# Attention's products with v and the state as moving operand, and chunk 0's w, k, r in 1,536-byte packets

## The chip, the cores and the metric

The kernel runs on one core of a Trainium2 chip. The metric is device time in microseconds, of the one core from launch to end; less is better. A core has TensorE (PE in the profile; PEld is its loading of the stationary operand, here called a load), VectorE (DVE), ScalarE (ACT), GpSimd (POOL) and SyncE (SP), which here sends the DMAs. Engines run side by side and wait for each other at semaphores. On each engine the instructions stand in a fixed order, written when the program is built.

In a product on TensorE one operand is loaded into the array and stays (stationary), the other streams through it (moving). In the profile's shapes `a<-m,v 128*64 128x128` the first pair is the loaded operand, rows by columns, and the second is the result's or the moving operand's, partitions by columns.

## The reference

An attention with a decaying state (4 batches, 8 heads, 768 tokens, head size 48), and an FFN with a squared ReLU on its result (3,072 tokens, 384 to 2,048 to 384), all in float32:

```python
for t in range(S):
    kt, vt, rt, wt = (k[:, :, t], v[:, :, t], r[:, :, t], w[:, :, t])
    cur = np.einsum('bhd,bhe->bhde', u[None] * kt, vt)
    y[:, :, t] = np.einsum('bhd,bhde->bhe', rt, state + cur)
    state = wt[:, :, :, None] * state + np.einsum('bhd,bhe->bhde', kt, vt)
...
x = np.ascontiguousarray(attn_out.transpose(0, 2, 1, 3)).reshape(B * S, H * D)
h = np.maximum(x @ w_in, 0.0)
return (h * h @ w_out).astype(np.float32)
```

## The kernel before, in words

**Tiling.** The 768 tokens of each batch are cut into 6 chunks of 128 (`C`). A *unit* is one chunk of one batch: 24 units, 4 a chunk. Heads go in 4 pairs (`NP`); in the layout "head dims on partitions" the pair's first head lies on partitions 0 to 47 and the second on 64 to 111 (`J` = 64, `D` = 48, `HP` = 112). Behind each chunk of attention comes the FFN of its 512 tokens: 16 steps of 128 hidden columns each. A step has 9 products with w_in (`hp`, L640; three products of rounded halves for each of 3 row blocks), a squared ReLU with a split into two rounded halves (ACT and DVE, L645 to L649), and 3 products with w_out for each batch (`ob`, L655). The first 6 steps of chunk 0 and all of chunk 1 are done in two halves of 2 batches.

**A unit.** (1) w, k, r arrive with tokens on partitions (`st`, L423) and must be turned. In chunk 0 that is four transposes a tensor on TensorE (`turn`, L466), in the later chunks a block transpose on DVE (L432) and DMAs that spread the blocks (L442). (2) DVE multiplies the decays up along the tokens (`scan`, L478) and, with ACT's reciprocal (L485, L486), scales r (L489) and k (L495 to L498). (3) `beta`, the sum over a head of u k r for each token, comes from two products on POOL (L505, L507) and a sum on DVE (L508); ACT writes it onto the diagonal of `m` (L515). (4) TensorE makes the scores of 128 by 128 tokens for each head (L526), DVE copies their causal part into `m` (L530). (5) The *mix* makes y: state times r (`inter`, L552) and v times scores (`part`, L560), summed in one PSUM tile `a`. v or the state is loaded (48 columns, or 64 with 16 of the head before), and 128 columns of r or scores move, so y comes out with head dims on partitions and the tokens along the row, as the FFN needs x. (6) ACT and DVE split y into the rounded halves of x (L591, L592). (7) The new state: k is turned to tokens (`ktok`, L538, L540), multiplied with v (`outer`, L611; 64 or 48 columns of k loaded, 48 columns of v moving) and added (L617 to L620).

Four pairs of 96 head dims must become three tiles of 128 rows. Pair 1 is therefore split: its dims are put on the 16 free partitions at either side of the other three pairs. In chunk 0 a copy `ly` (L577) and products with 0/1 matrices (`sel`, L574) do that on TensorE, later a tile `x3` and six DMAs for two units (`send`, L599). Rows of w_in are loaded in the same order, in five pieces a group (L370).

**Weights.** w_in and w_out come in 8 groups (`ri`, `ro`: 768 KB each) and are split into two rounded halves on the chip: ACT (L383, L403), DVE (L387, L391, L396) and POOL (L404).

**What sets the order.** The class `Plan` simulates the engines with the costs that stand in each `P.add(...)` and writes out an order for each engine; `Ranks` holds tables of numbers by which it prefers one step to another. Where the plan expects TensorE to be idle in the first 110 us, it puts in transposes of the unit matrix (L681) that keep its clock up. PSUM has 8 banks: 4 for the outputs `ob`, 2 for `hp`, 2 for `a`. In chunk 0 the `ob` and `hp` banks hold turned w, k, r as well.

Of the kernel before, what the change touches and what calls it, by code (L numbers as in the profile page):

```python
# [35 lines left out]
class Plan:  # L36
# [9 lines left out]
    LANES, RUNS, SLACK, START = 8, 2300, 2.0, 2.4  # L46
# [142 lines left out]
class Ranks:  # L189
    AT = {'load': -105.75, 'z': 279.5, 'pt': 293.75, 'rk': -330.75, 'beta': 21.25, 'far': 18.25, 'v': 60.25, 'scan': 43, 'ln': 19.75, 'rt': 19.5, 'kn': 51, 'diag': -5.25, 'mt': -159, 'mask': 173.5, 'ktp': -201.5, 'kt': 16.25, 'mix': 5.25, 'x': -131, 'x3': -22.5, 'send': 36, 'dS': 23, 'S': 10.5}  # L190
    AT0 = {'load': -89.75, 'turn': 101.5, 'rk': -33, 'beta': 11.5, 'far': 133.25, 'v': -15.75, 'scan': -196.25, 'ln': -291, 'rt': -31, 'kn': 99.25, 'diag': 45.5, 'mt': -172.75, 'mask': -100.5, 'ktp': 40.25, 'kt': 29.25, 'mix': -212, 'x': 187.5, 'x3': 11, 'send': 93, 'dS': -48, 'S': -101}
    AT1 = {'load': -20.75, 'z': -9.75, 'pt': -57, 'rk': -13, 'beta': 104.5, 'far': 35.25, 'v': -5.75, 'scan': -5.25, 'ln': -68, 'rt': -39.75, 'kn': 2, 'diag': 120.5, 'mt': -311.5, 'mask': -60.25, 'ktp': -46.5, 'kt': -83, 'mix': -111.75, 'x': -6.75, 'x3': -270.75, 'send': -105.75, 'dS': -29.75, 'S': 8.75}
    U0 = (-64.5, -118.75, -8.75, -25)
    C1 = (9.25, 16.75, 53.25, 46)
    W0 = (-110.25, -66.25, -12, 2.25, 3.25, 5, 8.25, 20)
    WL = (-20.5, 13, -41.5, -13, -1, 8.75, 20, 11.5)
    OFF = {'hp': 2.75, 'g': -5.75, 'ob': 4, 'os': 64.5}
    LAG = 2
# [25 lines left out]
def kernel(  # L224
# [46 lines left out]
    PC = J - D  # L271
    TILES, SPLIT = (0, 2, 3), 1
    SIDE = ((0, 0), (2, 1), (1, 2))
    spare, spare2 = placed[f"ro{NG - 2}"], placed[f"ri{NG - 2}"]
    sel = place("sel", [HP, KT, J], F32, spare)
    last_y = [place(f"ly{i}", [HP, C], F32, spare + 768 + 512 * i) for i in range(2)]
    first_v = [place(f"v0{i}", [128, H * J], F32, at) for i, at in enumerate((spare + 1792, spare + 3840, spare2, spare2 + 2048))]
# [28 lines left out]
    for t in st0:  # L306
        V.memset(t[:, :, :, :, D:J], 1.0)
# [34 lines left out]
    for t in first_v:  # L342
        V.memset(t.rearrange("s (h x) -> s h x", h=H)[:, :, 0:PC], 0.0)
# [4 lines left out]
    for t in Ss:  # L348
        V.memset(t, 0.0)
# [436 lines left out]
```

## Time and profile before

| | |
|---|---|
| median of 3 runs | 549.76 us (549.22 to 550.37) |
| the profiled execution | 549.26 us, of which 547.3 us are its span |
| granted TensorE clock, mean | 0.996 |
| DMA | 206,456 packets, 50.88 MB; 196,161 of them under 512 bytes |
| POOL in the first 40 us | busy between 0 and 4.7 us of each 5 |

A row of groups names the line, the engine, the operation, the tiles (out<-in, buffer numbers left out), the shapes and the count; behind the first bar stand the busy time in us (overlaps counted once) and the mean duration of one in ns, behind the second the idle time of the engine ahead of these instructions and what ended it. A row of the timeline has start and length in us, then a run of like instructions with its count. Records of TensorE overlap: one lasts some 200 to 400 ns, while the next starts well before it ends. A float32 product is two records for each instruction of the program; the FFN's products and the transposes are one.

### The profile page before, as it was taken

To read this page: it belongs to the slowest core of one execution; us is meant where nothing else is said; L and a number is where in the kernel's file an instruction comes from. 1 tells how busy PE (TensorE), PEld (TensorE's weight loads), DVE (VectorE), ACT (ScalarE), POOL (GpSimd) and SP (SyncE) were. 2 spreads that over 40 slices of the span, in tenths; PEclk is the share of its full clock that TensorE was granted. 3 is DMA by queue.
4 is the path that set the end of the run, shared out by engine and by line. 5 is a ranking of instruction groups with operands and counts; after the bars stand their busy time and mean duration, and the time that the engine had idled before them with its cause. 6 is when DMAs were issued, how large, how long until landed. Compare 5 with 4: busy or idle time off the path is not lost. (4 is left out here: it accounts for less than half of the span.)

```text
span 547.3 us, 10350 instructions
## 1 busy us (share of the span) xinstructions
PE 532.6 (97%) x3930; PEld 474.5 (87%) x3930; DVE 357.1 (65%) x650; ACT 287.3 (52%) x677; POOL 102.3 (19%) x119
## 2 busy tenths in 40 slices
PE   7899999999999999999999999999999999999995
PEld 6778988889998989888888888888888889899994
DVE  5889989999587775958667747656855332333331
ACT  2886885566855845655643654545553332332322
POOL 5335653540212020210302002003000000000000
PEclk9999999999999999999999999999999999999998
DMA  9999699156563825455553723703411000000001
GB/s 164 216 244 272 128 245 206 24 90 136 115 132 64 169 47 105 97 104 99 101 107 62 138 73 60 142 3 73 74 57 30 1 0 16 29 31 1 0 1 62
DMA packets 206456, 50.88 MB, mean 93 GB/s; under 512 B 196161, under 2 KB 201281, under 8 KB 206401
## 3 DMA queue, kind: packets, MB, share of 16 engines
q1 hardware_dynamic: 205680, 49.17, 44.0%
q10 hardware_dynamic: 720, 0.98, 0.6%
q8 instruction: 33, 0.54, 0.4%
q14 instruction: 23, 0.18, 0.1%
HBM read 31.65 MB, written 4.72 MB: 66 GB/s over the span
## 5 line engine op out<-in xcount | busy, mean ns | idle before, releaser
L655 PE MATMUL ob<-wo,g 128*128 128x384 f32 x1152 | 226.9, 341 | 0.5 <-ACT g L648 0.5
L640 PE MATMUL hp<-x,wi 128*128 128x512 f32 (+1 forms) x1062 | 222.7, 355 | 1.4 <-DVE g L649 0.9
L655 PEld LDWEIGHTS ob<-wo,g 128*128 128x128 f32 x1152 | 199.3, 188 | 9.2 <-ACT g L648 0.7
L640 PEld LDWEIGHTS hp<-x,wi 128*128 128x128 f32 x1062 | 174.5, 188 | 27.5 <-DVE g L649 2.3
L645 ACT ACTIVATE t<-hp 128x512 f32<-128x512 f32 (+1 forms) x118 | 61.1, 518 | 154.2 <-PE hp L640 132.5
L646 DVE SCALAR_TENSOR_TENSOR hp<-hp,t 128x512 f32<-128x512 f32 (+1 forms) x118 | 70.3, 596 | 102.0 <-ACT t L645 101.5
L649 DVE TENSOR_TENSOR g<-hp,g 128x512 fp32r<-128x512 f32 (+1 forms) x118 | 68.9, 585 | 38.1 <-ACT g L648 37.3
L648 ACT CAST g<-hp 128x512 fp32r<-128x512 f32 (+1 forms) x118 | 59.5, 505 | 55.7 <-DVE hp L646 55.6
L515 ACT ACTIVATE m<-ident,beta 128x128 f32<-128x128 f32 x192 | 60.4, 395 | 1.2 <-DVE beta L508 1.2
L505 POOL TENSOR_TENSOR st<-st 128x384 f32<-128x384 f32 x24 | 26.6, 1108 | 61.7 <-DVE st L432 54.5
L620 POOL TENSOR_TENSOR S<-S,Ec 112x192 f32<-112x192 f32 x16 | 8.3, 523 | 142.2 <-DVE S L619 142.2
L530 DVE COPY_PREDICATED m<-caus,a 128x512 f32<-128x512 uint8 x48 | 33.3, 730 | 0.7 <-PE a L526 0.6
L478 DVE TENSOR_TENSOR_SCAN pt<-pt,zero 112x128 f32<-112x128 f32 x80 | 30.3, 426 | 3.0 <-DMA v<-in_v_dram 1.3
L526 PEld LDWEIGHTS a<-pt 48*128 48x128 f32 x384 | 23.6, 187 | 7.3 <-issue 5.1
L526 PE MATMUL a<-pt 48*128 48x128 f32 x384 | 28.3, 285 | 1.1 <-DVE pt L498 1.1
L560 PE MATMUL a<-m,v 128*48 128x128 f32 (+1 forms) x384 | 27.2, 279 | 1.0 <-DVE m L530 1.0
L432 DVE STREAM_TRANSPOSE st<-st 128x1152 f32<-128x1152 f32 x20 | 27.2, 1366 | 0.0
L560 PEld LDWEIGHTS a<-m,v 128*48 128x48 f32 (+1 forms) x384 | 20.0, 128 | 6.4 <-issue 4.6
L592 DVE SCALAR_TENSOR_TENSOR x<-a,x 112x128 fp32r<-112x128 f32 (+2 forms) x44 | 17.5, 431 | 12.3 <-ACT x L591 11.7
L507 POOL TENSOR_TENSOR st<-st,un 128x384 f32<-128x384 f32 x24 | 25.1, 1047 | 1.6
L404 POOL TENSOR_TENSOR wi<-q,wi 128x768 fp32r<-128x768 f32 x8 | 17.6, 2204 | 38.0 <-ACT wi L403 31.5
L495 DVE TENSOR_TENSOR pt<-pt,m 112x512 f32<-112x512 f32 x24 | 17.4, 728 | 8.9 <-ACT m L486 8.3
(78 smaller groups left out, 417.1 us busy)
## 6 DMA issues: line engine op xcount, KB each, us to landing
pt<-st SPq DMA_DIRECT2D x80, 96.0 KB, 2.3
ro<-in_moe_w_out_dram SPq DMA_DIRECT2D x8, 768.0 KB, 7.5
v<-in_v_dram SPq DMA_DIRECT2D x24, 192.0 KB, 3.4
st<-in_w_dram SPq DMA_DIRECT2D x11, 384.0 KB, 4.2
st<-in_k_dram SPq DMA_DIRECT2D x11, 384.0 KB, 5.4
st<-in_r_dram SPq DMA_DIRECT2D x11, 384.0 KB, 5.6
pt<-st SPq DMA_DIRECT2D x80, 48.0 KB, 2.5
out_dram<-q SPq DMA_DIRECT2D x20, 192.0 KB, 1.9
```

The lines of the kernel that those rows point to most:

```text
L432: V.transpose(out=zt[:, i].rearrange("a t p q i -> a t (p q) i"), in_=sv[:, :, i].rearrange("s t p q x -> s t (p q) x"))
L478: lambda p=p: V.tensor_tensor_scan(out=pt[:, 0, p], data0=src(0)[:, p], data1=zero.broadcast_to([HP, C]), initial=1.0, op0=ALU.mult, op1=A ...
L515: A.activation(mv(j)[:, p], ident, AF.Copy, scale=beta.tile[:, 2 * p + j:2 * p + j + 1])
L526: T.matmul(mts[j].tile.rearrange("s (p t) -> s p t", p=NP)[:, p], pt[js, 2, p], pt[js, 1, p], start=True, stop=True)
L530: lambda j=j: V.copy_predicated(out=mv(j), mask=caus.unsqueeze(1).broadcast_to([128, NP, C]), data=mts[j].tile.rearrange("s (p t) -> s p t ...
L560: T.matmul(ybv()[to:to + n + D, spot(p)], vt.tile[:, o - n:o + D], mv(j)[:, p], start=(c == 0 and p == SPLIT), stop=True, skip_group_check ...
L640: T.matmul(hp.tile[:, 0:n], wi[f][:, wl, kt], xT[:, kt, xl, xs], start=(m == 0), stop=(m == 3 * KT - 1))
L645: P.add("act", 0.5 if full else 0.28, rank("g"), lambda: A.activation(t(), h(), AF.Relu), r=[hp], w=[(g, 1)])
L646: P.add("dve", 0.61 if full else 0.33, rank("g"), lambda: V.scalar_tensor_tensor(out=h(), in0=h(), scalar=0.0, in1=t(), op0=ALU.max, op1=A ...
L648: P.add("act", 0.53 if full else 0.31, rank("g"), lambda: A.copy(out=hi(), in_=h()), r=[hp], w=[(g, 0)])
L649: P.add("dve", 0.61 if full else 0.33, rank("g"), lambda: V.tensor_tensor(out=lo(), in0=h(), in1=hi().bitcast(F32), op=ALU.subtract), r=[h ...
L655: T.matmul(obs[b][:, 0:DM], g.tile[0][:, gl, o:o + C], wo[f][:, wl], start=(f == 0 and m == 0), stop=(f == NF - 1 and m == 2))
```

## The change

Two parts are rebuilt, and the tables of `Ranks` are other ones.

**The mix.** `part` now loads the scores (128 rows, 128 columns) and moves v (48 columns); `inter` loads r (48 rows, 128 columns) and moves the state (48 columns). y comes out with tokens on partitions and the 384 head dims along the row, in one PSUM tile in chunk 0 and in two (one for each head of a pair) later. ACT copies it to `ys` (with the sign), TensorE turns `ys` by three transposes (`back`), and ACT and DVE split the result into x. With that the 16-partition shifts go: `sel`, `ly`, `x3`, the six DMAs, w_in's row order and its five pieces.

**Chunk 0's w, k, r.** A DMA now puts 8 tokens of one head, 1,536 contiguous bytes, on a partition (head and block of 16 on the partitions), where before each token's 192 bytes were a packet. `turn` therefore isn't a transpose: for each of the 8 tokens y and each head of a pair, 64 or 48 columns are loaded and 64 picked columns of the unit matrix move; results go to every eighth column of the turned tile. `beta` of chunk 0 is made from the turned k and r: a copy on ACT, a product on DVE, four products with u on TensorE (`sums`), and a copy on ACT. In the later chunks it stays on POOL and DVE.

```diff
-    LANES, RUNS, SLACK, START = 8, 2300, 2.0, 2.4
+    LANES, RUNS, SLACK, START = 8, 2300, 2.0, 1.4
...
-    AT = {'load': -105.75, 'z': 279.5, 'pt': 293.75, 'rk': -330.75, ...
+    AT = {'load': -95.5, 'z': 119, 'pt': 209.75, 'rk': -91.75, ...
...
-        for i, (to, src) in enumerate(pieces):
-            n = 2 * PC if i >= KT else to.shape[0]
-            P.add("sp", 0.4 if i >= KT else 0.0059 * n, rank, lambda to=to, src=src: nc.sync.dma_start(out=to, in_=src),
-                  w=[("wi", g, i)], after=before, runs=n)
+        P.add("sp", 2.4, rank, lambda: nc.sync.dma_start(out=wi_r[g], in_=w_in32[g].rearrange("(k p) x -> p k x", p=128)),
+              w=[("wi", g, 0)], after=before if g == NG - 1 else [], runs=384)
...
+            for b0 in (b, b + 1) if c == 0 else ():
+                for i, src in ((0, w), (2, k), (1, r)):
+                    def load(i=i, src=src, b0=b0):
+                        nc.sync.dma_start(out=st.tile.rearrange("s (t b x) -> s t b x", t=3, b=2)[:, i, b0 - b, 0:TB * D],
+                                          in_=src[b0, :, ss, :].rearrange("h (a s) d -> h a (s d)", s=TB))
...
-                    for p in range(NP):
-                        T.transpose(out=to[:, p], in_=pairs[:, p], identity=ident)
-                P.add("pe", 0.5, rank("turn"), turn, r=[(st, ui, i)], w=[ps[i]])
+                    pick = ident.rearrange("s (p j x) -> s p j x", p=NP, j=2)
+                    for y in range(TB):
+                        for j in range(2):
+                            n = (J, D)[j]
+                            T.matmul(to[j * J:j * J + n, :, :, y], rows[:, y * D:y * D + n], pick[:, :, j], start=True, stop=True, skip_group_check=True)
+                P.add("pe", 1.0, rank("turn"), turn, r=[(st, ui, i)], w=[ps[i]], mode=3)
...
+        if c == 0:
+            P.add("act", 0.53, rank("rk"), lambda: A.activation(pt[:, 2], src(2), AF.Copy, scale=-1.0), r=keys(2), w=[PT[2]])
+            P.add("dve", 0.62, rank("rk"), lambda: V.tensor_tensor(out=pt[:, 2], in0=pt[:, 2], in1=src(1), op=ALU.mult), r=keys(1), w=[PT[2]])
+            def sums():
+                for p in range(NP):
+                    T.matmul(tl(ps[0])[:, 2 * p:2 * p + 2], pt[:, 2, p], ut[:, p], start=True, stop=True, skip_group_check=True)
+            P.add("pe", 0.45, rank("beta"), sums, r=[PT[2]], w=[ps[0]])
+            P.add("act", 0.2, rank("beta"), lambda: A.copy(out=beta.tile, in_=tl(ps[0])[:, 0:H]), r=[ps[0]], w=[beta])
...
-                    T.matmul(ybv()[j * J:j * J + n + D, spot(p)], Ss[b][js, PC + p * D - n:PC + p * D + D], pt[js, 1, p],
-                             start=(spot(p) == 0), stop=False, skip_group_check=True)
+                    T.matmul(place_of(p, j), pt[js, 1, p], Ss[b][js, p * D:p * D + D], start=(p == 0), stop=False, skip_group_check=True)
...
-                        T.matmul(ybv()[to:to + n + D, spot(p)], vt.tile[:, o - n:o + D], mv(j)[:, p],
-                                 start=(c == 0 and p == SPLIT), stop=True, skip_group_check=True)
+                    T.matmul(place_of(p, j), mv(j)[:, p], vt.tile[:, o:o + D], start=(c == 0 and o == 0), stop=True, skip_group_check=True)
...
+        if c:
+            P.add("pe", 0.45, rank("mix"), inter, r=[vt, *Ms, ("S", b), *RK], w=yb, mode=1)
+        P.add("pe", 0.75, rank("mix"), part, r=[vt, *Ms], w=yb)
...
+        def back():
+            for kt in range(KT):
+                T.transpose(out=xv()[:, kt], in_=ys.tile[:, kt * 128:kt * 128 + 128], identity=ident)
+        P.add("pe", 0.33, rank("y"), back, r=[(ys, j) for j in range(2 if c else 1)], w=[xp])
...
-                        nc.sync.dma_start(out=xT.bitcast(F32)[to:to + PC, q, :, b * C - C:b * C + C],
-                                          in_=x3.tile.bitcast(F32).rearrange("a z u c -> a z (u c)")[o:o + PC])
```

**What moves.** Lines of the changed kernel that the prediction names: L455 `turn`, L491 `sums`, L525 the scores, L550 `inter`, L556 `part`, L577 `back`, L537 `ktok`, L591 `outer`, L620 `hp`, L635 `ob`, L661 the transposes that keep the clock up; on DVE L467 the scan, L487 the product of chunk 0's `beta`, L478, L501, L502, L504 the scaling of r and k, L368, L372, L377 the weights' split, L529 the masked copy, L581 x, L597 the state.

TensorE in a steady unit, before (a are the two PSUM tiles, m the scores, v and S the values and the state, pt the scaled r and k; rows that alternate on are left out):

```order
L655 MATMUL ob_142<-wo_59,g_97 128x384 x3
L552 MATMUL a_145<-pt_127,S_130 64x128
L552 MATMUL a_145<-pt_127,S_130 48x128
...
L560 MATMUL a_145<-m_154,v_152 64x128
L560 MATMUL a_145<-m_159,v_152 48x128
...
L611 MATMUL a_146<-v_153,m_160 64x48
L611 MATMUL a_146<-v_153,m_160 48x48
...
L655 MATMUL ob_139<-wo_59,g_99 128x384 x3
```

The two mixes and the state's product stand in one block between FFN products. In the changed program, at such a unit (ys is the copied y):

```order
L635 MATMUL ob_143<-wo_67,g_94 128x384 x3
L550 MATMUL a_147<-S_128,pt_125 128x48
L550 MATMUL a_146<-S_128,pt_125 128x48
...
L620 MATMUL hp_144<-x_131,wi_73 128x512 x9
L556 MATMUL a_147<-v_154,m_159 128x48
L556 MATMUL a_146<-v_154,m_160 128x48
...
L635 MATMUL ob_140<-wo_71,g_92 128x384 x3
L635 MATMUL ob_141<-wo_71,g_92 128x384 x3
L577 MATMUL a_147<-ident,ys 128x128 x3
L537 MATMUL a_146<-ident,pt_125 128x112 x4
```

The block is taken apart, with FFN products between its pieces and ahead of the transposes that need ACT's copy; the results are 128 partitions by 48 columns instead of 64 or 48 by 128.

DVE ahead of the second unit's x, before (pt, m: decays and scaled r and k; x: the FFN's input; q: weights under way):

```order
L592 SCALAR_TENSOR_TENSOR x_134<-a_146,x_134 128x3x128
L478 SCALAR_TENSOR_TENSOR pt_128<-ob_141,zero 112x128 x4
L530 COPY_PREDICATED m_156<-caus,a_145 128x512
L530 COPY_PREDICATED m_157<-caus,a_146 128x512
L478 SCALAR_TENSOR_TENSOR pt_128<-ob_141,zero 112x128 x4
L489 TENSOR_TENSOR pt_128<-ob_142,pt_128 112x4x127
L508 TENSOR_REDUCE beta_168<-st_136 128x8
L495 TENSOR_TENSOR pt_128<-pt_128,m_155 112x512
L496 SCALAR_TENSOR_TENSOR m_155<-pt_128,m_155 112x512
L617 TENSOR_TENSOR S_129<-a_146,Ec_162 112x192
...
L592 SCALAR_TENSOR_TENSOR x_134<-a_145,x_134 128x3x128
```

Between the first unit's x and the second's stand both scans of the third and fourth unit. In the changed program:

```order
L581 TENSOR_TENSOR x_131<-a_146,x_131 128x3x128
L597 TENSOR_TENSOR S_126<-a_147,Ec_163 112x192
L368 TENSOR_SCALAR q_149<-q_149 128x768
L372 SCALAR_TENSOR_TENSOR q_149<-ri_56,q_149 128x768
L529 COPY_PREDICATED m_160<-caus,a_146 128x512
L529 COPY_PREDICATED m_161<-caus,a_147 128x512
L377 SCALAR_TENSOR_TENSOR q_149<-ri_56,q_149 128x768
L368 TENSOR_SCALAR q_148<-q_148 128x768
...
L478 TENSOR_TENSOR pt_125<-ob_143,pt_125 112x4x127
L581 TENSOR_TENSOR x_131<-a_147,x_131 128x3x128
```

There the weights' split (L368 to L377) and the third unit's scan stand between the two, and the fourth unit is not begun.

SP's first DMAs, before:

```order
L423 DMA st_135<-in_r_dram 128x8x48
L423 DMA st_135<-in_w_dram 128x8x48
L423 DMA st_135<-in_k_dram 128x8x48
L423 DMA st_135<-in_r_dram 128x8x48
L453 DMA v_91<-in_v_dram 128x8x48
L370 DMA ri_56<-in_moe_w_in_dram 112x512 x2
```

These follow the first unit's w and k; in the changed program the queue begins so:

```order
L404 DMA st_132<-in_w_dram 128x1x384
L404 DMA st_132<-in_k_dram 128x1x384
L404 DMA st_132<-in_r_dram 128x1x384
L351 DMA ri_60<-in_moe_w_in_dram 128x3x512
L353 DMA ro_62<-in_moe_w_out_dram 128x2x768
L404 DMA st_132<-in_w_dram 128x1x384
L404 DMA st_132<-in_k_dram 128x1x384
```

A group of weights, 1.5 MB, now stands ahead of the second unit's w.

More of the change, by code (lines that the diff above doesn't have):

```diff
@@ L268 @@
         wo_t.append(place(f"wo{g}", [128, 2, 2 * DM], F32R, placed[f"ro{g}"]))
[L271 to L277, printed above, removed]
+    spare = placed[f"ro{NG - 2}"]
+    first_v = [place(f"v0{i}", [128, DM], F32, spare + 4 * DM * i) for i in range(4)]
     gts = []
@@ L603, in attention @@
+        P.add("dve", 0.47, rank("x"), lambda: V.tensor_tensor(out=lo(), in0=xv(), in1=hi().bitcast(F32), op=ALU.subtract),
+              r=[xp, xk + ("hi",)], w=[xk + ("lo",)])
         if c < NC - 1:
@@ L735 @@
                     xp = pas[b % 2].rearrange("a (k s) -> a k s", s=C)[:, 0:KT]
[L737 removed]
                     for kt in range(KT):
[L739 to L744 removed]
+                        T.transpose(out=xp[:, kt], in_=xr[:, kt * 128:kt * 128 + 128], identity=ident)
                     hi, lo = (xT[:, :, z, b * C:b * C + C] for z in range(2))
```

164 lines of the change are left out of this document (61 added, 103 removed).

## The prediction

> **What bounds the kernel now.** I read the page first, then the windows of busy time, the waits of TensorE and the timeline of one steady unit; the chain that ended last came last.
>
> ```profile
> span 547.3 us, 10350 instructions
> PE 532.6 (97%) x3930; PEld 474.5 (87%) x3930; DVE 357.1 (65%) x650; ACT 287.3 (52%) x677; POOL 102.3 (19%) x119
> 1.60:34.70 33.10, 29.36 (x271) 24.71 (x271) 26.14 (x61) 20.35 (x54) 16.26 (x24) 1.00 1.11 216
> 34.70:80.00 45.30, 43.15 (x357) 38.67 (x358) 41.07 (x73) 36.71 (x87) 22.06 (x13) 1.00 0.91 213
> 80.00:420.00 340.00, 339.39 (x2653) 302.35 (x2652) 250.09 (x459) 192.66 (x472) 62.99 (x74) 1.00 0.48 95
> 420.00:540.00 120.00, 120.00 (x649) 108.15 (x648) 39.09 (x58) 35.35 (x64) 0.00 (x0) 1.00 0.03 9
> PE a L526 <- DVE pt L498: 0.3, 1, 0.3
> PE hp L640 <- DVE g L649: 0.3, 1, 0.3
> 542.41 0.48 ACT q L660
> ```
>
> The windows give, after the stretch and its length, the busy time of PE, PEld, DVE, ACT and POOL, then the granted clock (1.00 all along), the DMA share and GB/s. From 80 us on TensorE is busy in 459.39 of 460 us; the two rows of waits, taken from 80 us on, are all that it waits for, 0.6 us. So **behind 80 us the time is TensorE's own work**: whatever a unit of attention adds to TensorE comes out at the end, one for one, and nothing on DVE, ACT or the queues hides it. Before that the start is bound elsewhere: DVE has 26.14 of 33.10 us, and TensorE's 29.36 hold warming transposes of the unit matrix (L681). The chain view holds a last copy alone, since the kernel ends on a flag that is read back; it says nothing of the middle.
>
> **The change, part by part: the units behind chunk 0.** There are 20. One of them reads, on TensorE:
>
> ```profile
> 302.42 1.08 PE L552 MATMUL a<-pt,S 48*64 48x128 f32 x16
> 303.43 1.09 PE L560 MATMUL a<-m,v 128*64 128x128 f32 x16
> 304.35 0.62 PE L611 MATMUL a<-v,m 128*48 128x48 f32 x16
> 304.90 2.35 PE L655 MATMUL ob<-wo,g 128*128 128x384 f32 x12
> ...
> 314.91 1.16 PE L526 MATMUL a<-pt 48*128 48x128 f32 x16
> 316.00 0.44 PE L655 MATMUL ob<-wo,g 128*128 128x384 f32 x1
> ```
>
> Each of the 8 float32 products is two records. From start to start, L552 takes 1.01 us and L560 0.92: 1.93 us for both, and that is what goes away. In L560, v is loaded (48 or 64 columns) and 128 columns of scores move; two halves of the array work side by side. In the new form the scores are loaded (128 columns) and 48 columns of v move: **less moves, more is loaded, and no second half works beside it**. So what decides is what a load of 128 columns costs when little moves behind it.
>
> ```profile
> L611 PE MATMUL a<-v,m 128*64 128x48 f32 x160 | 12.4, 222 | 0.0
> L611 PE MATMUL a<-v,m 128*48 128x48 f32 x160 | 10.5, 210 | 0.0
> L611 PEld LDWEIGHTS a<-v,m 128*64 128x64 f32 x160 | 11.5, 138 | 1.3 <-issue 1.0 <-ACT m L540 0.2
> L611 PEld LDWEIGHTS a<-v,m 128*48 128x48 f32 x160 | 9.6, 124 | 0.0
> L694 PEld LDWEIGHTS a<-flag,ones 128*128 128x128 f32 x2 | 0.4, 188 | 0.0
> L694 PE MATMUL a<-flag,ones x2: 166/208/251, 540.4 to 540.4; 128*128 128x1 f32 x2
> 540.39 0.28 PE L694 MATMUL a<-flag,ones 128*128 128x1 f32 x2
> 12.21 4.31 PE L681 MATMUL a<-ident 128*128 128x128 f32 x38
> ```
>
> L611 is the state's product, and both its halves move the same 48 columns; one loads 64 columns, the other 48. In each of 20 units a half has 8 records, so its busy time is seven steps and one duration: (12.4/20 - 0.222)/7 = **0.057 us a step** with 64 columns loaded, (10.5/20 - 0.210)/7 = 0.045 with 48. The half that loads more is slower, so the load sets its pace, not what moves. The loads' own durations grow alike: 124, 138 and 188 ns at 48, 64 and 128 columns. L694 (the flag) is the one place where 128 float32 columns are loaded and next to nothing moves, one column: its two records are busy for 0.28 us, the first for 0.166, so the second ends 0.11 later. From 64 columns I come to the same: 0.057 + 64 x 0.012/16 = 0.105. I take **0.11 us for a record with 128 columns loaded**, however little moves.
>
> - L556, scores times v: 16 records one behind the other, 16 x 0.11 = 1.76 us. Bounds: 16 x 0.045 = 0.72, if the load were hidden, and 1.8 if each goes as a transpose of L681 does (4.31/38 = 0.113).
> - L550, r times state: 48 rows and 128 columns loaded, as L526 has them, in two row halves side by side. L526 takes 1.09 with a changeover behind it. I take 1.0; bounds 8 x 0.045 = 0.36 and 1.09.
> - L577, three transposes of the result, as L681: 3 x 0.113 = 0.34. Their wait for ACT's copy of y is covered by L635 and L620, which stand between in the order.
>
> Sum 3.10 against 1.93: +1.17 us a unit, **20 x 1.17 = +23.4 us**. By the bounds it is between 20 x (1.42 - 1.93) = -10 and 20 x (3.23 - 1.93) = +26. I stay near the upper end, since the nearest row (L694) is the very shape. Changeovers between whole and divided array are 131 and 135 in the two orders; at no more than 0.1 each that is +0.4. ACT's added copies of y and the removed DVE pieces, x3 and L599's transfers, lie beside a busy TensorE and cost or save nothing.
>
> The Trainium skill's page TensorE: Matmul & The Clock Gate has a rule that speaks for the change: by its section Back-to-back issue gap, 1 to 64 moving columns cost some 25 ns. As an estimate from that page L556 would be 16 x 0.025 = 0.4 us, L550 0.3 with its changeover, the unit 1.04 and the 20 units -18 us instead of +23.4. L611's step of 57 ns with 48 moving columns doesn't agree with it for float32 loads; it is the first rival below, priced there from rows.
>
> **The start.** What the first FFN product waits for:
>
> ```profile
> 0.82 0.45 SPq L423 DMA_DIRECT2D st<-in_w_dram  x1
> 6.08 0.89 PE L466 MATMUL ob<-ident,st 128*128 128x128 f32 x4
> 7.01 1.37 DVE L478 TENSOR_TENSOR_SCAN pt<-ob,zero 112x128 f32<-112x128 f32 x4 [2.81 <-PE ob L466]
> 7.00:35.30 28.30, 24.50 (x249) 20.03 (x248) 24.24 (x47) 20.41 (x54) 14.33 (x19) 1.00 1.15 228
> 34.71 0.38 PE L640 MATMUL hp<-x,wi 128*128 128x256 f32 x1 [0.26 <-ACT x L591]
> un<-in_u_dram ACTq DMA_DIRECT2D x1, 192.0 KB, 4.5
> out_dram<-q ACTq DMA_DIRECT2D x4, 192.0 KB, 2.3
> ```
>
> The first w is sent for at 0.82 and turned at 6.08; from the first scan (7.01) to the x of the second unit DVE has 24.24 us of work in 28.3. In the new order w comes in 128 pieces of 1,536 bytes. The nearest rows are u and the outputs, of the same size and pieces: 4.5 and 2.3 us to landing, so w lands at 3.1 to 5.3. Its turn is now 16 pairs with 64 and 48 columns loaded, at L611's 0.057: 0.91 us, where 4 transposes took 4 x 0.113 = 0.45. The first scan then starts between 4.1 and 6.4; I take 5.5, 1.5 earlier. Bounds of a turn: 16 x 0.045 = 0.72 and, if its scattered writes spoil the pairing, 32 x 0.057 = 1.8.
>
> ```profile
> L478 DVE TENSOR_TENSOR_SCAN pt<-ob,zero 112x128 f32<-112x128 f32 x16 | 5.4, 399 | 2.8 <-PE ob L466 2.8
> L530 DVE COPY_PREDICATED m<-caus,a 128x512 f32<-128x512 uint8 x4 | 2.8, 721 | 0.1
> L496 DVE SCALAR_TENSOR_TENSOR m<-pt,m 112x512 f32<-112x512 f32 x4 | 2.8, 688 | 0.1
> L592 DVE SCALAR_TENSOR_TENSOR x<-a,x 128x384 fp32r<-128x384 f32 x2 | 1.1, 558 | 1.6 <-ACT x L591 1.6
> L387 DVE TENSOR_SCALAR q<-q 128x768 uint32<-128x768 uint32 x2 | 1.1, 554 | 0.4 <-ACT q L383 0.4
> L391 DVE SCALAR_TENSOR_TENSOR q<-ri,q 128x768 uint32<-128x768 uint32 x1 | 1.0, 951 | 0.0
> ```
>
> From the first scan to the second unit's x the new order has on DVE: 12 scans (5.4/16 = 0.34), 11 products of 512 elements (0.69), 4 masks (0.72), 3 shifts (0.55), 5 bit merges (0.95), 2 x (0.56) and one state (0.36): 4.1 + 7.6 + 2.9 + 1.7 + 4.8 + 1.1 + 0.4 = 22.6 us, 1.6 less than now. With waits as now (28.3 - 24.2 = 4.1) that x, and with it the first FFN product, comes at 5.5 + 22.6 + 4.1 = 32.2, where it now is ready at 35.3 (28.3 behind 7.0): **3.1 earlier**.
>
> Behind it chunk 0 has more for TensorE than now: two turns and not one (2 x 0.91 - 0.45 = +1.4), two sums of r, k and u (L491, 8 records with 128 columns loaded, 0.88 each: +1.8), and two mixes at 1.76 + 0.34 = 2.1, where now stands
>
> ```profile
> 55.07 0.87 PE L574 MATMUL a<-ly,sel 48*64 48x128 f32 x12
> ...
> 56.57 0.62 PE L611 MATMUL a<-v,m 128*48 128x48 f32 x16
> ```
>
> 1.5 us and some 0.3 of an earlier piece: +0.6 for both. That is +3.8 against -3.1, so the start gives **+0.7**, between -4 (w lands early, waits vanish) and +7 (slow turns). The 34 warming transposes behind that point, now 25, fill waits and add none.
>
> **Sum.** The profiled execution took 549.26 us, 1.96 around its span; the median shown is 549.76, half a microsecond more, inside what I can tell. 549.3 + 23.4 + 0.4 + 0.7 = **573.8, say 574 us**.
>
> **Rivals.**
> - *The load hides behind the moving columns* (**not slower**). Were a record with 128 columns loaded as quick as L611's, 0.05, then L556 takes 0.8, L550 0.5, L577 0.34: 1.64, a gain of 0.29 a unit, 5.8 in all; the start gives -3.1 + 1.4 + 0.8 - 1.3 = -2.2. That is 549.3 - 5.8 - 2.2 + 0.4 = 542 us. It decides from a step of 0.062 us, where 24 steps, a changeover of 0.1 and the 0.34 of L577 make up the 1.93 of now. For it speaks that only two records in this trace have the new shape; against it L611's two halves.
> - *The turns are slow.* Their results go to every eighth element of PSUM, which nothing in this trace does. At 1.8 us a turn outlasts the 1.37 us of scans beside it, and from there it decides: four turns on the way to the first FFN product and two behind it, 6 x 0.9 = +5.4: 579 us. The Trainium skill's page Advanced Engine Details and Errata, section PSUM Cachelines, says that results which aren't contiguous slow matmuls significantly; no row here can show it.
> - *The start doesn't come earlier*, because the weights' large transfers stand right behind the first three and POOL and ACT are still late: the 3.1 us fall away, 577 us.
>
> **How the numbers follow.** Forecast 0.71, slow turns 0.09, no earlier start 0.06, hidden load 0.14 (of which 0.02 ends within 0.2% of now). A measurement of this kernel can tell about 0.2% from no change. So faster 0.12, same 0.02, slower 0.86. The forecast's own spread is 565 to 582 (unit sums 2.85 to 3.3, start -4 to +4); with the two slower rivals, 561 to 585 holds 0.8 and leaves out the hidden load.
>
> **What would show it.** In the new profile: L556 at about 1.8 us a unit and 0.11 a record, L550 at 1.0, L577 at 0.34; L455 at 0.9 a turn; the first L620 near 32; TensorE without waits behind 80 us. It is wrong if L556 takes under 1 us a unit, or if TensorE waits there for ACT's copies of y.

## The result, and the profile after

The changed kernel took 585.14 us (median of 4 runs, 583.16 to 586.84), the kernel before 550.07 on the same chip (549.22 to 551.24). That is 1.0635 times the time of before (95% interval 1.0594 to 1.0676): slower, as forecast, by 35 us where 24 were forecast. The profiled execution took 586.84 us, 585.1 of them its span. The profiled execution of block_inter below was a slow one (586.00 us, mean granted clock 0.987, against 577.09 to 579.76 us for its other four), so only its stretch at full clock is compared.

The windows of busy time of the changed kernel, in the columns shown for before (length, PE, PEld, DVE, ACT, POOL, granted clock, DMA share, GB/s):

```profile
1.60:34.70 33.10, 29.96 (x394) 27.74 (x394) 18.59 (x34) 17.30 (x42) 3.78 (x7) 0.95 0.81 233
34.70:80.00 45.30, 44.06 (x459) 40.56 (x458) 38.61 (x70) 33.18 (x75) 18.18 (x11) 0.96 0.79 224
80.00:420.00 340.00, 338.20 (x2510) 305.04 (x2510) 236.64 (x417) 191.14 (x477) 67.64 (x77) 1.00 0.51 81
420.00:540.00 120.00, 120.00 (x713) 107.17 (x713) 48.02 (x79) 44.51 (x92) 1.39 (x2) 1.00 0.09 23
```

and what TensorE waits for behind 80 us (in all, times, longest):

```profile
PE ob L635 <- DVE g L629: 1.0, 1, 1.0
PE hp L620 <- DVE g L629: 0.8, 1, 0.8
```

TensorE is as full as before: 338.20 of 340 us and 120 of 120, with 1.8 us of waits. More work was added to a full engine. In the first stretch POOL fell from 16.26 to 3.78 and DVE from 26.14 to 18.59, and neither made the start shorter. The clock column counts the time ahead of the first recorded change as full. That change is to full clock and came at 6.64 us before and at 19.73 after; until then the clock was half: in the changed kernel the 32 records of a turn take 1.97 us at 10.16 and 1.15 at 42.79 (both rows are below).

To see where the time came in, I count the records of the FFN's products (L620 and L635, before L640 and L655; 2,214 in both). The 200th is counted from 0 here, so 200 records lie ahead of it; behind its start 20 units of attention are left in both programs. It comes at 81.22 us before and at 92.12 after: **+10.9**. From there to the product of the flag it is 459.2 us before and 485.8 after: **+26.6**. Forecast were +0.7 and +23.8.

A later unit of the changed kernel, from its timeline on TensorE (start, length, then line, shapes and count):

```profile
296.27 2.26 PE L620 MATMUL hp<-x,wi 128*128 128x512 f32 x9
298.37 2.24 PE L635 MATMUL ob<-wo,g 128*128 128x384 f32 x12
300.45 2.26 PE L620 MATMUL hp<-x,wi 128*128 128x512 f32 x9
302.65 1.16 PE L525 MATMUL a<-pt 48*128 48x128 f32 x16
303.74 1.86 PE L635 MATMUL ob<-wo,g 128*128 128x384 f32 x9
305.53 1.09 PE L550 MATMUL a<-S,pt 48*128 48x48 f32 x16
306.56 0.80 PE L635 MATMUL ob<-wo,g 128*128 128x384 f32 x3
307.19 1.88 PE L556 MATMUL a<-v,m 128*128 128x48 f32 x16
308.89 2.35 PE L620 MATMUL hp<-x,wi 128*128 128x512 f32 x9
311.08 0.49 PE L577 MATMUL a<-ident,ys 128*128 128x128 f32 x3
311.40 0.55 PE L537 MATMUL a<-ident,pt 112*128 112x112 f32 x4
```

Starts are to be subtracted, since lengths overlap. L550 takes 305.53 to 306.56, 1.03; L556 takes 307.19 to 308.89, 1.70 (16 records, 0.106 each); L577 0.32. Together 3.05 us, where L552 and L560 took 1.93. The FFN records show a second cost. Undisturbed, 12 of L635 take 298.37 to 300.45, 2.08, so 0.173 each; the 9 ahead of L550 take 1.79 where 9 x 0.173 = 1.56, the 3 behind it 0.63 for 0.52, and the 9 of L620 behind L556 take 2.19 where undisturbed they take 2.10.

The start, first on DVE (in brackets the idle time ahead and what ended it):

```profile
6.70 1.36 DVE L467 TENSOR_TENSOR_SCAN pt<-ob,zero 112x128 f32<-112x128 f32 x4 [4.64 <-PE ob L455]
12.25 0.69 DVE L487 TENSOR_TENSOR pt<-pt,ob 112x512 f32<-112x512 f32 x1 [4.19 <-PE ob L455]
20.03 1.37 DVE L467 TENSOR_TENSOR_SCAN pt<-ob,zero 112x128 f32<-112x128 f32 x4 [1.95 <-PE ob L455]
37.77 0.56 DVE L581 TENSOR_TENSOR x<-a,x 128x384 fp32r<-128x384 f32 x1 [0.73 <-ACT x L580]
```

then on TensorE:

```profile
4.67 3.68 PE L455 MATMUL ob<-ident,st 128*64 128x64 f32 x64 [1.31 <-DMA st<-in_w_dram]
10.16 1.97 PE L455 MATMUL ob<-ident,st 128*64 128x64 f32 x32 [1.81 <-DMA st<-in_r_dram]
38.44 2.08 PE L455 MATMUL a<-ident,st 128*64 128x64 f32 x64
40.45 2.41 PE L620 MATMUL hp<-x,wi 128*128 128x256 f32 x18
42.79 1.15 PE L455 MATMUL ob<-ident,st 128*64 128x64 f32 x32
43.87 1.05 PE L491 MATMUL ob<-ut,pt 112*128 112x2 f32 x8
```

The first w is turned from 4.67 on, but the first r only from 10.16 on, so the product behind it (L487) waits 4.19 us. The second unit's x is ready at 38.33, and the first FFN product stands behind two more turns, until 40.45. At half clock two turns take 3.68 us (first row), at full clock 2.08 (third row).

### The profile page after: what moved, and what is told of

The parts are those of the page before. It is cut to its first block, busy times and chain, and to the rows that moved or that the text cites. A ratio compares the mean times of both kernels' runs of the same rounds, so it can differ in the third digit from the quotient of the medians.

```text
span 585.1 us, 10795 instructions
## 1 busy us (share of the span) xinstructions
PE 570.4 (97%) x4269; PEld 515.8 (88%) x4269; DVE 354.1 (61%) x620; ACT 298.7 (51%) x705; POOL 91.9 (16%) x104
## 5 line engine op out<-in xcount | busy, mean ns | idle before, releaser
L635 PE MATMUL ob<-wo,g 128*128 128x384 f32 x1152 | 234.2, 344 | 1.5 <-DVE g L629 1.0
L620 PE MATMUL hp<-x,wi 128*128 128x512 f32 (+1 forms) x1062 | 224.0, 356 | 1.1 <-DVE g L629 0.8
L635 PEld LDWEIGHTS ob<-wo,g 128*128 128x128 f32 x1152 | 199.1, 189 | 9.9 <-DVE g L629 1.3
L620 PEld LDWEIGHTS hp<-x,wi 128*128 128x128 f32 x1062 | 174.0, 188 | 27.0 <-DVE g L629 2.3
L556 PEld LDWEIGHTS a<-v,m 128*128 128x128 f32 x384 | 46.3, 192 | 1.0 <-DVE m L529 0.3
L556 PE MATMUL a<-v,m 128*128 128x48 f32 x384 | 46.1, 272 | 0.2 <-DVE m L529 0.2
L529 DVE COPY_PREDICATED m<-caus,a 128x512 f32<-128x512 uint8 x48 | 33.2, 733 | 13.1 <-PE a L525 10.9
L568 ACT ACTIVATE ys<-a 128x192 f32<-128x192 f32 x40 | 11.1, 330 | 51.7 <-PE a L556 51.7
L496 POOL TENSOR_TENSOR st<-st 128x384 f32<-128x384 f32 x20 | 22.1, 1107 | 79.2 <-DVE st L419 79.2
L467 DVE TENSOR_TENSOR_SCAN pt<-pt,zero 112x128 f32<-112x128 f32 x80 | 29.1, 406 | 1.4 <-DMA out_dram<-q 1.1
L525 PEld LDWEIGHTS a<-pt 48*128 48x128 f32 x384 | 23.4, 187 | 5.9 <-issue 2.4
L525 PE MATMUL a<-pt 48*128 48x128 f32 x384 | 28.0, 285 | 0.0
L581 DVE TENSOR_TENSOR x<-a,x 128x384 fp32r<-128x384 f32 x24 | 13.3, 555 | 22.6 <-ACT x L580 22.5
L550 PEld LDWEIGHTS a<-S,pt 48*128 48x128 f32 x320 | 19.4, 187 | 5.5 <-issue 3.9
L385 POOL TENSOR_TENSOR wi<-q,wi 128x768 fp32r<-128x768 f32 x8 | 16.3, 2041 | 41.2 <-ACT wi L384 41.2
```

The costliest lines, as they stand in the source:

```text
L467: lambda p=p: V.tensor_tensor_scan(out=pt[:, 0, p], data0=src(0)[:, p], data1=zero.broadcast_to([HP, C]), initial=1.0, op0=ALU.mult, op1=A ...
L525: T.matmul(mts[j].tile.rearrange("s (p t) -> s p t", p=NP)[:, p], pt[js, 2, p], pt[js, 1, p], start=True, stop=True)
L529: lambda j=j: V.copy_predicated(out=mv(j), mask=caus.unsqueeze(1).broadcast_to([128, NP, C]), data=mts[j].tile.rearrange("s (p t) -> s p t ...
L556: T.matmul(place_of(p, j), mv(j)[:, p], vt.tile[:, o:o + D], start=(c == 0 and o == 0), stop=True, skip_group_check=True)
L620: T.matmul(hp.tile[:, 0:n], wi[f][:, wl, kt], xT[:, kt, xl, xs], start=(m == 0), stop=(m == 3 * KT - 1))
L635: T.matmul(obs[b][:, 0:DM], g.tile[0][:, gl, o:o + C], wo[f][:, wl], start=(f == 0 and m == 0), stop=(f == NF - 1 and m == 2))
```

## The experiments

All of them start from the changed kernel except where it is said. The first FFN product and the 200th FFN record are starts in the profiled execution; the last column runs from there to the flag's product. Each ratio is to the kernel before on the same chip; for the runs below `after` that one took 550.55 to 551.04 us.

| kernel | median us | ratio to before (95%) | first FFN product | 200th FFN record | from there |
|---|---|---|---|---|---|
| before | 550.07 | | 34.71 | 81.22 | 459.2 |
| after | 585.14 | 1.0594 to 1.0676 | 40.45 | 92.12 | 485.8 |
| wide_v | 584.68 | 1.0560 to 1.0632 | 40.38 | 91.99 | 485.8 |
| extra_whole | 588.32 | 1.0619 to 1.0699 | 38.72 | 90.39 | 489.1 |
| extra_divided | 593.19 | 1.0746 to 1.0811 | 38.05 | 88.18 | 495.0 |
| block_inter | 579.70 | 1.0478 to 1.0538 | 40.27 | 92.29 | 483.3 |
| mix_only | 588.69 | 1.0646 to 1.0708 | 33.22 | 93.20 | 486.8 |
| loads_only | 577.23 | 1.0436 to 1.0505 | 47.23 | 107.82 | 459.2 |
| fill | 583.46 | 1.0564 to 1.0626 | 38.93 | 89.00 | 485.8 |
| late_w | 588.08 | 1.0618 to 1.0684 | 44.20 | 94.31 | 485.7 |
| late_w_fill | 590.44 | 1.0684 to 1.0742 | 43.87 | 95.59 | 485.8 |
| late_split | 588.73 | 1.0665 to 1.0707 | 45.06 | 96.73 | 485.8 |
| sums_twice | 586.01 | 1.0592 to 1.0710 | 39.73 | 91.42 | 485.8 |

The last column is the steadiest number here: 485.7 to 485.8 in six kernels whose starts differ by 8 us. It is read for the units, the two columns ahead of it for the start.

**Does the load or what moves set the pace?** Twice as many columns of v move:

```diff
-                    T.matmul(place_of(p, j), mv(j)[:, p], vt.tile[:, o:o + D], start=(c == 0 and o == 0), stop=True, skip_group_check=True)
+                    T.matmul(place_of(p, j, WV), mv(j)[:, p], vt.tile[:, min(o, DM - WV):min(o, DM - WV) + WV], start=(c == 0 and o == 0), stop=True, skip_group_check=True)
```

(WV = 96 behind chunk 0; 48 of the 96 columns aren't read, and the last head's are its neighbour's.)

> The changed kernel, but in the later chunks each product of scores with v moves 96 columns instead of 48 (the second 48 are another head's and go to columns nobody reads; of the last head the values read are its neighbour's). Load theory: a record is paced by its 128 loaded columns at 0.112 us, and 96 moving columns still hide behind that, so the line keeps its 0.112 us a record and the time stays at that of the changed kernel, 585 us within 2. Rival, pace set by what moves: 48 more columns at L611's streaming are 0.04 us a record, 16 records, 20 units: +13 us, 598.

Its timeline on TensorE, in the same unit:

```profile
307.08 1.92 PE L558 MATMUL a<-v,m 128*128 128x96 f32 x16
308.78 2.34 PE L622 MATMUL hp<-x,wi 128*128 128x512 f32 x9
```

1.70 us for 16 records with 96 moving columns, the same as with 48, and 485.8 for 485.8 in all. With up to 96 columns moving, the load sets the pace.

**What does it cost to divide the array?** One more product in each later unit ahead of the transposes of y, once with 128 loaded rows, once with 48:

```diff
+            if c:
+                T.matmul(xp.tile[:, 400:402], ident, ident[:, 0:2], start=True, stop=True, skip_group_check=True)
```

> The changed kernel with one more product ahead of the transposes of y in each of the 20 later units: the whole unit matrix loaded, two columns moving, into columns nobody reads. Control for the next: two records of 0.112 us a unit, 20 units, +4.5 us, 589 to 590, whatever a changeover costs.

> The same extra product, but with 48 rows loaded instead of 128, so that the array is divided for it. Changeover theory: one stretch of divided array between whole ones costs 0.3 us (0.1 on the way in, 0.1 on the way out, 0.1 at the second record behind it), 20 units, +6 us over the control: 595 to 596. As the prediction had it, 0.1 a changeover and two of them: +4, 593 to 594. No cost: as the control.

Timeline of the one with 128 rows, from the FFN records ahead of the product to the transposes:

```profile
308.94 2.35 PE L622 MATMUL hp<-x,wi 128*128 128x512 f32 x9
311.12 0.28 PE L577 MATMUL a<-ident 128*128 128x2 f32 x2
311.26 0.53 PE L579 MATMUL a<-ident,ys 128*128 128x128 f32 x3
311.62 0.55 PE L537 MATMUL a<-ident,pt 112*128 112x112 f32 x4
```

and of the one with 48:

```profile
310.02 2.35 PE L622 MATMUL hp<-x,wi 128*128 128x512 f32 x9
312.30 0.38 PE L577 MATMUL a<-ident 48*128 48x2 f32 x2
312.61 0.55 PE L579 MATMUL a<-ident,ys 128*128 128x128 f32 x3
313.00 0.55 PE L537 MATMUL a<-ident,pt 112*128 112x112 f32 x4
```

The same FFN records take 2.18 ahead of the whole array and 2.28 ahead of the divided one (+0.10, the way in); the product's two records 0.14 and 0.31 (+0.17, with the way out); the transposes 0.36 and 0.39 (+0.03). That is 0.30 us for one excursion. Over the 20 units: 495.0 - 489.1 = 5.9 us, 0.295 each. The section Key Properties of the page TensorEngine Tiling (Array Packing) in the Trainium skill says that changing the tiling mode drains TensorE; these rows agree with it, at 0.30 us for one excursion. The medians, 593.19 and 588.32, are only 4.9 us apart, and 593.19 is what two changeovers of 0.1 were to give; but the first 80 us, where the clock differs between the two executions, are in them. The control cost 3.3 us in all, not the 4.5 expected.

**The same cost taken away.** In two of the four batches the state is held as blocks of 96 by 96 (112 rows, zeros in the other head's place), so that `inter` needs no divided array:

```diff
+                if block:
+                    o = 2 * p * D
+                    T.matmul(yb[0].tile[:, o:o + 2 * D], pt[:, 1, p], Ss[b][:, o:o + 2 * D], start=(p == 0), stop=False, skip_group_check=True)
```

> The changed kernel, where in the two later batches the state is held as 96x96 blocks (112 rows, the other head's place zero), so that r times state is four whole-array products with 96 moving columns instead of eight with 48 loaded rows; the state's two updates go in two halves of rows there. In 10 of the 20 later units one divided stretch of the array is gone. Theory (a divided stretch between whole-array products costs 0.30 us beside its records): 8 records at 0.106 to 0.112 = 0.85 to 0.90 for 1.03, and 0.30 less around them: 0.43 to 0.48 a unit, 4.3 to 4.8 in all, the time 580 to 581. Rival (changes of the array's division are free, the records alone count): 0.13 to 0.18 a unit, the time 583.4 to 584. In the trace the two kinds of unit stand side by side: the FFN records next to the state's product keep 95 to 105 ns of excess each in the one and lose it in the other.

Its timeline at such a unit:

```profile
302.81 1.86 PE L644 MATMUL ob<-wo,g 128*128 128x384 f32 x9
304.50 1.03 PE L553 MATMUL a<-S,pt 112*128 112x96 f32 x8
305.31 0.77 PE L644 MATMUL ob<-wo,g 128*128 128x384 f32 x3
305.92 1.88 PE L562 MATMUL a<-v,m 128*128 128x48 f32 x16
```

Against the unit of the changed kernel the 9 records ahead take 1.69 for 1.79, the product 0.81 for 1.03, the 3 behind 0.61 for 0.63: 0.34 less, 3.4 for 10 units. The gain in all is 485.8 - 483.3 = 2.5; two waits of the scores inside (at 174 and 362 us, 0.43 and 0.24) explain most of the difference. My 4.3 to 4.8 was too high: the 3 records behind had little to give back. The rival's 1.3 to 1.8 is too low. The median fell by more than these 2.5, but with it the start varies, so that it isn't the measure here.

**One part of the change alone.** mix_only has the new mix with the start of before; loads_only has the kernel before with the new loads, turns and `beta` of chunk 0, and its old tables. Both orders were made by tables written for another program.

> Half of the change: the new mix with the new tables, but chunk 0's w, k, r, their turning and beta as before (planned anew, start cost as before). If the loads of 128 columns and the third divided stretch a unit make the loss behind 80 us, and chunk 0's new transfers and turns the late start, this one has the loss of the later chunks (20 units x 1.05, and 20 x 0.3) and a start within 2 us of before: 549 + 27 = 576 us, first FFN product near 35. If the mix itself makes the start late (longer chain from the masks to x): 582 or more, first FFN product near 40.

> The other half: the kernel before with chunk 0's w, k, r in 1,536-byte packets, the new turning and beta, and the tables of before (planned anew with the new costs). If what is late in the changed kernel's start is the new loads' doing (six more us to the first FFN product, and some 4 us of turns and sums behind it): 553 to 559 us. If the late start comes from the order of the queue alone, which the tables of before set otherwise, the packets bring it forward: 545 to 549.

Both totals missed both theories. From the 200th FFN record on the answer is clean: mix_only has 486.8, 27.6 more than before where its first theory had 27, and loads_only 459.2, so **the whole loss behind the start is the mix's, and the loads add nothing there**. The starts, 93.20 and 107.82, were spoilt by things of their own. The first FFN product of mix_only came at 33.22, earlier than before, so the new mix alone does not make that one late; behind it TensorE waited 5.9 us for g (written on DVE) and worked at half clock from 40.15 to 43.57 and from 50.39 to 64.05. What TensorE waited for in loads_only in its first 60 us, the two longest:

```profile
PE ob L481 <- DMA st<-in_w_dram: 3.5, 2, 2.1
PE a L599 <- ACT ly L602: 2.7, 1, 2.7
```

So neither says what its part could do at the start in an order made for it.

**The clock at the start.** 20 more warming transposes ahead of the first turn:

```diff
+            if first and s.engine == "pe":
+                n, first = n + 20, False
```

> The changed kernel with 20 more transposes of the unit matrix ahead of the first turn, nothing else moved. Clock theory: TensorE works at half clock until 19.7 us because seven transposes and waits are too little activity; with 27 the full clock is granted before 10 us, the turns and transposes until 20 us take half as long and the first FFN product comes 2 to 4 us earlier: 581 to 583. Queue theory: the start waits for r and the second unit's transfers, a faster TensorE waits for the same: 585, and it is 585 or 586 if the added transposes only delay the first turn.

In this trace the clock was full from 6.39 us on, as before (6.64). In the changed kernel it was full only from 19.73 on, and half again from 26.55 to 29.97 and from 64.1 to 67.5. The 200th FFN record came 3.1 us earlier, at 89.00, though the first scan came later (8.22 for 6.70), behind the longer row of transposes. That the added transposes brought the full clock isn't shown: extra_divided, with seven as in the changed kernel, had it from 12.81 on without a break, and its record came at 88.18. Nor do the medians tell (583.46 for 585.14, with intervals that overlap). What the two executions show is the start at nearly full clock: 7.0 to 7.8 of the 10.9 us stay, so the clock isn't the main cause. The windows up to the 200th FFN record, on TensorE (PE and PEld), first all of it and then three lines of it, before (L466 turns, L681 warming transposes):

```profile
0.00:81.22 81.22, 73.73 (x635) 64.42 (x635) 68.96 (x134) 58.83 (x141) 40.50 (x46) 1.00 0.97 211
0.00:81.22 81.22, 7.78 (x48) 5.44 (x48) 1.00 0.97 211
0.00:81.22 81.22, 19.54 (x130) 16.48 (x130) 1.00 0.97 211
```

and in fill (L459 turns, L495 sums, L665 warming transposes):

```profile
0.00:89.00 89.00, 80.35 (x933) 73.67 (x933) 68.27 (x122) 56.62 (x127) 29.76 (x31) 1.00 0.78 211
0.00:89.00 89.00, 13.25 (x384) 11.94 (x384) 1.00 0.78 211
0.00:89.00 89.00, 4.13 (x32) 3.88 (x32) 1.00 0.78 211
0.00:89.00 89.00, 15.40 (x97) 13.39 (x97) 1.00 0.78 211
```

Turns +5.5, sums +4.1, the rest of attention and FFN +1.2 (80.35 less the other three, against before). Warming transposes gave back 4.1, idle time grew by 1.2. That is the +7.8 lost, within rounding. So chunk 0's work moved onto TensorE is 9.6 us, and fewer warming transposes made up for 4.1 of it. This is a count; by itself it doesn't show that the work, and not the waits for it, set the time.

**More work at the start.** To test this, the sums are done twice in fill:

```diff
-                for p in range(NP):
+                for p in (*range(NP), *range(NP)):
```

> The run fill (the changed kernel with 20 more warming transposes ahead of the first turn) with the products that sum r, k and u over the channels done twice in each of the four units of chunk 0, to the same places: 32 more records, 0.9 us a unit at full clock, 3.6 us in all. Theory (up to some 90 us TensorE has little slack left, so that work added there shows in the time): two to four units' worth shows, the 200th FFN record comes at 91 to 92.5 us (89.0 in fill) and the time is 585.5 to 587. Rival (the start is a chain of DVE, ACT and transfers, and TensorE's work beside it is hidden as the warming transposes are): the 200th FFN record within 0.7 us of 89.0, the time 583 to 584.5.

The 200th FFN record came 2.4 us later, inside the theory's band. Of that, 0.8 arose ahead of the first FFN product and 1.6 behind it, where two units' sums stand (1.8). The trace bears the theory out behind that point; ahead of it, and in the median (582.82 to 589.91), it can't be settled, because the clock was half from 23.25 to 30.07 in this execution and full in fill's.

**Can the chain of the first two units come earlier?** In the changed kernel two weight transfers of 768 KB stand on SP behind the first three loads. late_w sends them behind the second unit's w, k and r, late_w_fill adds the 20 transposes, late_split also moves the unpacking of those weights:

```diff
+            sp = [s for s in out if s.engine == "sp"]
+            big = [s for s in sp[:6] if s.runs in (384, 256)]
...
+            i = out.index(sp[7]) + 1
+            out[i:i] = big
...
+            self.hold = self.hold[1:] + self.hold[:1]
+            for s in self.hold:
+                out.remove(s)
+            i = out.index(self.anchor) + 1
+            out[i:i] = self.hold
```

> The changed kernel with one edit on SP's queue: the first group of weights (two transfers of 768 KB) is sent for behind the second unit's w, k, r instead of ahead of them. Queue theory: r of the first unit then lands near 5 us instead of 10, DVE's wait of 4.2 us there goes, the second unit's data are there in time, and the first FFN product comes 3 to 5 us earlier: 580 to 582. Clock theory: the late landing is covered anyway by slow turns: 584 to 585.

> Both edits of the two runs before. If each takes away its own part of the late start, the first FFN product is near 33 and the time 577 to 579; if one hides behind the other, no better than the better one of them.

> This is late_w_fill (both weight transfers of the first group behind the second unit's w, k, r; 20 more warming transposes) with one thing more: the unpacking of the first 768 KB of input weights on ACT, DVE and POOL, and ACT's first unpacking step of the next 768 KB, stand in the order behind the first unit's state update, not ahead of the first unit's r and k products. In late_w_fill ACT stood 5.13 us and DVE 5.04 us before these steps, waiting for the weights. Theory (the start is bound by the chain of the first two units on DVE, and the moved transfers gave nothing there because the unpacking, in the queue ahead of that chain, waited for them): DVE no longer stands between 12 and 17 us, TensorE's first scores come near 15 us (20.7 there), the first FFN product near 32 to 34 us (43.9 there, 38.9 in the run with the warming transposes alone), and the time is 576.5 to 579. Rival (something else holds the start, the landing of v or of the next weights, or TensorE's own chain): the first FFN product at 37 us or later, the time 582 or more.

All three missed their theories, by 6 to 11 us. Of the alternatives, late_split's came true (45.06, and 588.73), which names no single cause, and late_w_fill is no better than the better of its two. DVE in late_w_fill:

```profile
9.83 0.69 DVE L502 TENSOR_TENSOR pt<-pt,ob 112x512 f32<-112x512 f32 x1 [0.57 <-PE ob L470]
17.30 0.56 DVE L383 TENSOR_SCALAR q<-q 128x768 uint32<-128x768 uint32 x1 [5.04 <-ACT q L379]
```

The wait for r (4.19) is gone, and L502 (L487 in the changed kernel) comes at 9.83 instead of 12.25. But the next in the queue is the unpacking of weights that now land later, and DVE stands 5.04 us there. In late_split that is mended, and its scores stood at 16.21 where the changed kernel's stood at 20.84. Then it lost the gain again, on ACT:

```profile
26.50 0.89 ACT L388 ACTIVATE q<-ri 128x768 f32<-128x768 f32 x1
30.06 0.83 ACT L408 CAST wi<-q 128x768 fp32r<-128x768 f32 x1 [2.67 <-DVE q L401]
31.59 1.26 ACT L540 ACTIVATE m<-ident,beta 128x128 f32<-128x128 f32 x4
```

The second unit's diagonal (L540, its other half at 25.32) now stood behind the unpacking. And TensorE ran at half clock from 21.56 to 28.38 and from 35.21 to 42.04, in late_w from 17.97 to 35.03 and in late_w_fill from 19.39 to 33.04, where fill had full clock. In each of the three a wait for the unpacking stood in the chain (4.06 and 5.04 us on DVE, 2.67 on ACT), but how much of their loss is that and how much the clock wasn't separated.

## Why the prediction was right, and where not

The direction, the place (TensorE behind 80 us) and the largest term were right for the reason given. The total was not: 24 us were forecast and 35 came, from two terms that were mis-sized. That 585.14 still falls at the very end of the stated range, 561 to 585, is luck: that end was drawn for turns slowed by their scattered writes. The first four turns were that slow, 1.8 to 2.0 us each, but at half clock.

*Behind 80 us the time is TensorE's own work.* Right. Its waits there are 1.8 us; the extra products of extra_whole and extra_divided came out in the time (3.3 and 9.2 us in the last column).

*0.11 us for a record with 128 loaded columns, however little moves.* Right. It measured 0.106, L556 1.70 (1.76 forecast), L550 1.03 (1.0), L577 0.32 (0.34); wide_v shows that 48 more moving columns cost nothing. So the rival of the hidden load falls. The 25 ns of the Trainium skill (page TensorE: Matmul & The Clock Gate, section Back-to-back issue gap) belong there to an isolated product; in a stream of loads and products, by the same section, both set the spacing, and the 0.106 us here agree with that. The prediction read the figure as one for such a stream. Summed over the trace from each start to the next, the mix of the 20 units grew by 21.0 us where 23.4 were forecast.

*Changeovers, +0.4.* This step failed, first in its count. 131 and 135 are changes from any division of the array to any other, among them those inside one block, from `inter` to `part` to `outer`. Between the whole array and a divided one, which the prediction named, the traces have 102 before and 132 after: at its own 0.1 each, +3.0. And the price is another one, too: TensorE pays each time that it goes from the FFN's products into the divided array, and each time that it comes back to them from other products. Before, `inter`, `part` and `outer` stood in one block; after, they are three stretches with FFN products between. I counted, behind the 200th FFN record, 54 returns to FFN products before and 99 after; the first record behind a return is 0.08 us longer behind whole-array products and some 0.11 behind divided ones, which makes 4.1 us more. The way into the divided array, 0.09 to 0.10 each, comes 52 times for 40: 1.0 more. FFN records took 5.4 us more in all; with the mix's 21.0 and 0.3 of the rest that is, within rounding, the 26.6. extra_divided and block_inter show the price of an excursion by adding and removing one. The price of a return from whole-array products is counted, not tested by a run, and no run put the three stretches back into one block.

*The start, +0.7.* This is the other step that failed; it measured +10.9 in the profiled execution. Of its parts the landing of w (3.1 to 5.3; turned at 4.67) and DVE's work (22.6; 21.57, the time from 6.70 to 38.33 without the waits) were right. The first scan came at 6.70, not 5.5, mostly because the turns ran at half clock. DVE's waits were 10.06 us (4.19, 1.95 and 0.73 above, and five others of 3.2 in all), not 4.1: I carried the waits of before over. 6.5 us of them ended with TensorE's turns and sums, 4.19 of that behind the late r, and 3.6 with ACT. That makes 6.70 + 21.57 + 10.06 = 38.33, and the two turns ahead of L620 make 40.45, for a forecast of 32.2. I also took the clock of before for granted, without a reason: up to the 200th record 26.6 us stood at half clock after the change, 6.6 before. With the clock nearly full, in fill, DVE still waited 6.9 us up to the second unit's x, 3.0 for turns and sums and 4.0 for ACT. Behind the first FFN product I had +3.8 of work; fill measured 50.07 us from there to the 200th record against 46.51 before, +3.6, and there I was right.

*The rival of slow turns* falls. At full clock 32 records of a turn take 42.79 to 43.87, 1.08 with the change of division, for 0.91 forecast; the writes to every eighth element don't double it. The section PSUM Cachelines of the Trainium skill's page Advanced Engine Details and Errata spoke for that rival; of the slowing that it names, at most these 0.17 us a turn can be seen here. *The rival of no earlier start* named the place, the weights' transfers behind the first loads, but priced it at 3 us. Moving them away (late_w) brought no earlier start, so how early the start could come is **still open**: no run brought the first FFN product of the whole change before 38.0 us.

The sum of 574 was 11 us short: +2.8 from the units, +10.2 from the start, less the 1.7 by which the profiled execution exceeds the median.

## What to carry to other kernels

A float32 product with few moving columns costs what its load costs: choose as the loaded operand the one with fewer columns, and let the many move. On a full TensorE a step that is cut into pieces pays some 0.1 us each time that it returns to the main product and up to 0.3 each time that it divides the array in between, so count the interruptions. Work taken off POOL and DVE onto TensorE is free only as far as warming transposes give way to it: here 4.1 us of 9.6.

## What was not expected of the hardware

The clock fell to half without idle time. Windows of the changed kernel, each 3.41 us, the one ahead of the drop and the one behind it:

```profile
23.14:26.55 3.41, 3.39 (x31) 3.27 (x32) 2.90 (x6) 1.40 (x4) 0.00 (x0) 1.00 0.80 256
26.55:29.97 3.42, 3.42 (x29) 3.00 (x27) 2.96 (x5) 3.36 (x11) 0.00 (x0) 0.50 1.07 243
```

TensorE was busy in 3.39 of 3.41 us, by 31 records, 24 of which moved few columns (L556 with 48, the sums with 2; the other 7 are transposes), and got half the clock for the next 3.41. In mix_only it was busy in all 13.66 us from 50.39 to 64.05 and stayed at half clock throughout. In fill a stretch with 2.02 of 3.41 us busy was followed by full clock:

```profile
13.21:16.62 3.41, 2.02 (x18) 1.78 (x18) 3.28 (x6) 3.38 (x11) 0.00 (x0) 1.00 0.67 193
16.62:20.03 3.41, 3.21 (x80) 2.99 (x80) 2.32 (x6) 2.71 (x6) 1.49 (x1) 1.00 0.53 99
```

The Trainium skill's page TensorE: Matmul & The Clock Gate, section What's actually happening, gives windows of 3.4 us, which fits these lengths, and lets idle windows bring the half clock, which doesn't fit the first pair. What brings it was not settled; with the same seven warming transposes the full clock first came at 7.88 us (extra_whole), 9.74 (block_inter), 12.81 (extra_divided) and 19.73 (the changed kernel).
